# Inverse roots of the first four tiles by square root and reciprocal, one operand for the k and v weights, a last VectorE batch of four, and output stores on two queues

## The chip, the core and the metric

The kernel runs on one core of a Trainium2 chip. The metric is the time of one execution on the device, in microseconds (us); lower is better. The time of the kernel before is the median of three runs. Profiles show one further execution each, with their own time.

## What is computed

`x` has 2048 rows (tokens) of 512 numbers, in bf16. Two branches work on its layer-normalised form:

```python
xn = layernorm(x)                       # (x - mean) / sqrt(var + 1e-5)
q = (xn @ wq) as 32 heads of 16         # one k and one v for all heads
k, v = xn @ wk, xn @ wv                 # wk, wv: 512 x 16
p = softmax(q @ k.T * 16**-0.5)         # 32 heads x 2048 x 2048
s = (p @ v as 2048 x 512) @ wo
g = silu(silu(xn @ w1) @ w2)            # 512 -> 1792 -> 512
out = x + s * g
```

The exponentials of the softmax are by far the most elements: 32 x 2048 x 2048.

## The kernel before, in words

The five engines run programs that a planner inside the kernel file writes out. `Planner` (L108) keeps a clock for each engine; the code adds `Task`s with an engine, an expected duration, what they read and write and a priority, and the loop at L1856 always lets the engine with the lowest clock take its next task. The result is a fixed order for each engine, with semaphore waits where one engine needs another's result (`finalize`, L272; `run_engine`, L333). The expected durations only decide the order; on the chip each engine goes through its list as fast as its waits allow. The planner's thresholds are varied at random in each 6 us of planned time (`Mix.draw`, L349), from a list of seeds (`SEEDS`, L23; a seed of 0 leaves the base values). Another list of seeds, or another task, gives another order everywhere behind it.

**Exponentials.** The work is cut into 32 groups (16 blocks of queries and heads, twice) of 64 slots, so 2048 slots. One slot is a 128x512 block of scores that TensorE writes to one PSUM bank by four 64x32 matmuls (`score`, L1020). Each slot's exponential is made in one of two ways:

- On ScalarE (ACT): one `Exp` at L1804 over one bank, or over two banks at once, into `pa_sb`. TensorE then multiplies it with v, two matmuls a slot (L1382).
- On VectorE (DVE): one `tensor_scalar` at L1113 (L1833 for two banks) into `db_sb` makes bf16 bits of an approximate power. Three shifted copies of it, each over a whole batch, are added as integers on GpSimd (POOL, L1300) or, late in the run, on DVE (L1296), into `ds_sb`. All four are multiplied with differently weighted v and summed by TensorE, so a slot costs eight matmuls at L1382. Slots go to DVE in batches of `BS` = 8 (`pick_d`, L1080). A batch is begun only in a group with `MARGIN` (24, varied by the seeds) or more slots left, in the last group `MARGIN_END` (24). What is not taken by DVE goes to ACT.

**Start.** Four x tiles of 128 tokens are loaded first. DVE makes their mean and variance (L578, L582; tile 1 on ACT, L566 to L571), then the inverse root of variance + eps by a bit trick and two Newton steps: eight dependent DVE instructions a chain (L595 to L604), one chain for tiles 0 and 1, one for 2 and 3 (`FIRST`, L44), later ones for eight and four tiles. Then `xn` (L607), transposes on TensorE (L646), their evacuation (L656 on ACT, L657 on DVE), k by L681 and q by L793, then the first scores (L1035) and the first `Exp`. TensorE runs matmuls on zeros (L1757) until the first transposes. ACT's table load and a first `Exp` of one column stand at L557.

The k product takes 32 columns of weights for each quarter of the array from `wke_sb`, which ACT fills with eight copies of `wk` (L559). The evacuation of k multiplies with `part_sb`, a mask that keeps the first 16 rows of every other 32 and makes the others zero. The v product reads `wv_sb` (L719).

**End.** After the last `Exp` come the last products with v, the normalisation by DVE (L1403 to L1424), the last block of `wo` (L630), and for four output tiles r = 0 to 3 the gate and the residual: r = 0 and 1 by sums on TensorE (L1654) and a copy on ACT (L1657), r = 2 and 3 by an addition on DVE (L1668). Each then goes out by one 128 KB DMA from SyncE (SP) through `store` (L860, L861).

```python
tail["sums"] = [(r, part) for part in (1, 0) for r in PES]   # PES = (1, 0)
```

Of the kernel before, what the change touches and what calls it, by code (L numbers as in the profile page):

```python
# [15 lines left out]
P = 128  # L16
# [6 lines left out]
SEEDS, STRETCH = [0, 0, 107193, 696001, 868130, 0, 0, 145354, 0, 0, 0, 0, 659755, 570515, 0, 401028, 149754, 476048, 392543, 420941, 806026, 839768, 568520, 820467, 562019, 44193, 553940, 622483, 698310, 0, 0, 544188, 92220, 709879, 0, 0, 0, 801168, 299022, 0, 917407, 348101, 0, 418696, 641980, 788014, 105079, 62529, 143744, 620893, 549519, 710614, 527239, 0, 717222, 643687, 714474, 0, 598637, 596527, 685847, 646319, 190982, 346243, 377627, 0, 742035, 0, 484115, 974384, 0, 500386, 117077, 477174, 734943, 6340, 727301, 977691, 161521, 875247, 810658, 479061, 572316, 817044, 687626, 0, 340370, 623436, 215637, 14408, 0, 304983, 649749, 270166, 85731, 904261, 0, 0, 0, 0, 0, 9294, 415416, 179748, 0, 0, 265034, 0, 0], 6000.0  # L23
# [22 lines left out]
T_SP = 600.0  # L46
# [17 lines left out]
MARGIN, MARGIN_END = 24, 24  # L64
# [309 lines left out]
def bass_recurrent_scan__grouped_kv_mqa__dense_activation_silu__prompt_kernel(  # L374
# [29 lines left out]
    with ExitStack() as es:  # L404
# [6 lines left out]
        wk_sb = sb("wk_sb", [P, NDC, DH], BF16)  # L411
        wke_sb = sb("wke_sb", [P, NDC, P], BF16)
        wv_sb = sb("wv_sb", [P, NDC, DH], BF16)
# [72 lines left out]
        dma(SP, "wk", wk_sb[:], A_wk.rearrange("(dc p) e -> p dc e", p=P), 16, ["wk"], prio=0)  # L486
        dma(SP, "wv", wv_sb[:], A_wv.rearrange("(dc p) e -> p dc e", p=P), 16, ["wv"], prio=0)
# [19 lines left out]
        pl.add(Task(DV, 60.0, lambda v: v.memset(scr_sb[:], 0.0), (), ["scr"], -1))  # L507
# [41 lines left out]
        for e in (1, 0):  # L549
# [7 lines left out]
        pl.add(Task(AC, 1500.0, lambda a: a.activation(scr_sb[:, 0:1], scr_sb[:, 1:2], ACT.Exp), ["scr"], ["scr2"], 0))  # L557
        wke4 = wke_sb[:].rearrange("p c (i e) -> p c i e", e=DH)
        pl.add(Task(AC, 500.0, lambda a: a.activation(  # L559
            wke4, wk_sb[:, :, :].unsqueeze(2).to_broadcast([P, NDC, 8, DH]), ACT.Copy),  # L560
            ["wk"], ["wke"], 1, gate=lambda: "scr2" in pl.lastw and ("mv", 1) in pl.lastw))

# [24 lines left out]
        for n in first:  # L587
# [5 lines left out]
            def dv(fn, reads, writes, pre, ports=1):  # L593
                return pl.add(Task(DV, 66.0, fn, reads, writes, g, [pre] if pre is not None else [], ports=ports))
            t = pl.add(Task(DV, 66.0, lambda v, a=a, b=b, w=w: v.tensor_scalar(  # L595
                w, mv_sb[:, a:b, 1], LN_EPS, None, op0=ALU.add), [("mv", i) for i in tiles], [("ve", a)], g,
                [aggr[i] for i in tiles], ports=2))
            t = dv(lambda v, y=y, w=w: v.tensor_scalar(
                y.bitcast(I32), w.bitcast(I32), -0.5, RSQRT_M, op0=ALU.mult, op1=ALU.add), [("ve", a)], [("rs", a)], t, 2)
            for it, (c0, c1) in enumerate(RSQRT_C):  # L600
                t = dv(lambda v, y=y, h=h, c0=c0: v.scalar_tensor_tensor(
                    out=h, in0=y, scalar=c0, in1=y, op0=ALU.mult, op1=ALU.mult), [("rs", a)], [("vh", a)], t)
                t = dv(lambda v, w=w, h=h: v.tensor_tensor(h, h, w, ALU.mult), [("ve", a), ("vh", a)], [("vh", a)], t)
                t = dv(lambda v, y=y, h=h, c1=c1: v.scalar_tensor_tensor(  # L604
                    out=y, in0=h, scalar=c1, in1=y, op0=ALU.add, op1=ALU.mult), [("rs", a), ("vh", a)], [("rs", a)], t)
# [68 lines left out]
        def mk_K(c, ka, kb, bk=None):  # L674
            n = (kb - ka) * P

            def rnd(dc):
                def mk(b):
                    def emit(pe):
                        for j in range(4):  # L680
                            h = pe.matmul(bank(b)[32 * j:32 * (j + 1), 0:n], lhsT=wke_sb[:, dc, 32 * j:32 * (j + 1)],  # L681
                                          rhs=xnT_sb[:, dc, ka * P:kb * P], start=dc == 0, stop=dc == NDC - 1,
                                          tile_position=(0, 32 * j), skip_group_check=True)
                        return h
                    return emit
                return mk
# [20 lines left out]
            jb = job("K", c, 0.0, [(rnd(dc), ["wke"] + keys, max(64.0, n / 2.4 + 3.0)) for dc in range(NDC)], consume,  # L707
                     bk=bk, gate=lambda: all(k in pl.lastw for k in keys))
            if KU and n == NQ:
                product(jb, lambda k, rows, a, n: wke_sb[rows, k, a:a + n], lambda k, rows: xnT_sb[rows, k, ka * P:kb * P],  # L710
                        lambda k: ["wke"] + keys)

        def mk_V(c):
            def rnd(k):
                def mk(b):
                    def emit(pe):
                        for t in range(2 * k, 2 * k + 2):
                            for dc in range(NDC):
                                h = pe.matmul(bank(b)[:, t * DH:(t + 1) * DH], lhsT=xnT_sb[:, dc, (4 * c + t) * P:(4 * c + t + 1) * P],  # L719
                                              rhs=wv_sb[:, dc, :], start=dc == 0, stop=dc == NDC - 1, skip_group_check=True)  # L720
# [139 lines left out]
        def store(tt, t2):  # L860
            return pl.add(Task(SP, T_SP, lambda e: e.dma_start(of.rearrange("(t p) d -> p t d", p=P)[:, tt, :], ob_sb[:, tt % 4, :]),  # L861
# [188 lines left out]
        def pool_backlog():  # L1050
            return sum(t.dur for t in pl.tasks[PO] if t.dur == T_P64) + pl.clk[PO] - pl.clk[PE]
# [27 lines left out]

        def pick_d(t):  # L1080
            if st["assigned"] < 8 or any(k not in evac_kt or evac_kt[k].op is None for k in range(DK)):
                return None
            for bt in batches:
                for k in sorted(range(BS), key=lambda k: not mated(bt.g, k % 2)):
                    if k not in bt.slots and slot_time(bt.g, k % 2) <= t + 20:
                        return bt, k
            if any(len(bt.slots) < BS for bt in batches) or pool_backlog() > mix.P_HIGH:
# [848 lines left out]
```

## Time and profile before

| What | us |
|---|---|
| Median of three runs | 656.87 |
| Lowest and highest | 656.49, 657.04 |
| The profiled execution's own time | 657.56 |
| Its span, first to last instruction | 655.7 |
| Busy in it: TensorE (PE), ScalarE (ACT), VectorE (DVE), GpSimd (POOL) | 647.9, 641.0, 631.0, 576.5 |
| First `Exp` of scores starts | 12.00 |
| Last output store issued by | 653.78 |

A line of the profile's timeline has the start, the length of the piece, the engine, the line in the kernel, the operation, what it writes and reads, and how many instructions are merged in it; in brackets stands the idle time of the engine before it and what ended that. PEld is TensorE's loading of weights, SPq the queue on which SyncE issues DMAs. The granted TensorE clock is 1.0 in the whole span.

### The profile page before, as it was taken

The page shows a single profiled execution, that of the slowest core. Times are in us where ns is not written, and L with a number is a line of the kernel's source. Part 1 is how long each engine was busy: PE and PEld are TensorE (multiplying, and loading weights), DVE is VectorE, ACT ScalarE, POOL GpSimd, SP SyncE. Part 2 cuts the span into 40 slices and gives each one's busy share as a digit, 9 for nine tenths or more (in the row PEclk, how much of TensorE's full clock was granted, in tenths as well). Part 3 has the DMA queues.
Part 4 walks back from the last instruction along what each step waited for, and adds up shares of the span by engine and source line. Part 5 has one row for each costly group of instructions (what it writes and reads, how often), then busy time and mean ns, then how long its engine had stood idle before and what let it go on. Part 6 is the DMA issues. An engine that isn't in the chain of part 4 may idle for free.

```text
span 655.7 us, 44308 instructions
## 1 busy us (share of the span) xinstructions
PE 647.9 (99%) x21992; PEld 351.0 (54%) x19464; DVE 631.0 (96%) x1147; ACT 641.0 (98%) x1124; POOL 576.5 (88%) x330
## 2 busy tenths in 40 slices
PE   8999999999999999999999999999999999999997
PEld 4444456556544555554455556454665555665552
DVE  8999999999999999999999999999999999999992
ACT  6999999999999999999999999999999999999996
POOL 3069889999999999999999999999989999998950
PEclk9999999999999999999999999999999999999999
DMA  6521110000011210000000001000000001200001
GB/s 176 159 59 34 51 36 21 10 5 10 4 43 36 36 28 19 10 4 4 12 4 10 12 12 27 4 4 10 5 10 4 10 12 22 44 10 4 5 4 34
DMA packets 12937, 16.58 MB, mean 25 GB/s; under 512 B 2448, under 2 KB 11920, under 8 KB 12560
## 3 DMA queue, kind: packets, MB, share of 16 engines
q1 hardware_dynamic: 10544, 11.44, 5.9%
q0 software_dynamic: 1920, 2.03, 2.4%
q8 instruction: 162, 2.65, 1.7%
q10 hardware_dynamic: 288, 0.26, 0.1%
q14 instruction: 23, 0.19, 0.1%
HBM read 8.95 MB, written 3.67 MB: 19 GB/s over the span
## 4 chain that ended last, share of the span: by engine, by line
PE 86%; ACT 12%; DVE 2%; issue 0%
PE ps L1382 29%; PE ps L1035 25%; PE ps L757 18%; ACT pa_sb L1804 11%; PE ps L1029 11%; PE ps L1757 1%; DVE stats_sb L578 1%; PE ps L1614 1%; PE ps L646 0%; PE ps L681 0%; ACT t_sb L813 0%; PE ps L719 0%; DVE w_sb L852 0%; DVE xnT_sb L657 0%; DVE xn_sb L607 0%
## 5 line engine op out<-in xcount | busy, mean ns | idle before, releaser
L1804 ACT ACTIVATE pa_sb<-ps 128x512 bf16<-128x512 f32 (+1 forms) x1034 | 610.7, 765 | 3.3 <-PE ps L1035 2.8
L1300 POOL INT64_ADD ds_sb<-db_sb x298 | 562.2, 1961 | 29.6 <-DVE db_sb L1113 9.7
L1113 DVE TENSOR_SCALAR db_sb<-ps 128x512 uint16<-128x512 f32 x798 | 495.6, 680 | 3.8 <-PE ps L1035 1.0
L1035 PE MATMUL ps<-qt_sb,kt_sb 64*32 64x512 bf16 x5664 | 478.8, 378 | 0.7 <-DVE kt_sb L699 0.3
L1382 PE MATMUL ps<-ds_sb,v_sb 64*32 64x512 bf16 x4848 | 358.7, 376 | 0.0
L1382 PE MATMUL ps<-pa_sb,v_sb 64*32 64x512 bf16 x2480 | 264.4, 377 | 0.1
L1029 PE MATMUL ps<-qt_sb,kt_sb 64*32 64x512 bf16 x2528 | 243.7, 375 | 0.6 <-ACT pa_sb L1804 0.3
L1035 PEld LDWEIGHTS ps<-qt_sb,kt_sb 64*32 64x32 bf16 x5664 | 136.8, 89 | 141.0 <-ACT pa_sb L1804 55.9
L1382 PE MATMUL ps<-db_sb,v_sb 64*32 64x512 bf16 x1616 | 192.9, 376 | 0.0
L1382 PEld LDWEIGHTS ps<-ds_sb,v_sb 64*32 64x32 bf16 x4848 | 142.8, 91 | 44.4 <-issue 10.4
L757 PE MATMUL ps<-w_sb,u_sb 64*32 64x512 bf16 x1792 | 135.7, 377 | 0.0
L757 PE MATMUL ps<-xnT_sb,w_sb 64*32 64x512 bf16 x1792 | 135.2, 377 | 0.0
L1382 PEld LDWEIGHTS ps<-pa_sb,v_sb 64*32 64x32 bf16 x2480 | 91.1, 91 | 31.7 <-issue 10.8
L1382 PEld LDWEIGHTS ps<-db_sb,v_sb 64*32 64x32 bf16 x1616 | 64.5, 91 | 14.0 <-issue 2.4
L757 PEld LDWEIGHTS ps<-xnT_sb,w_sb 64*32 64x32 bf16 x1792 | 43.3, 91 | 24.2 <-issue 5.6
L757 PEld LDWEIGHTS ps<-w_sb,u_sb 64*32 64x32 bf16 x1792 | 46.2, 92 | 17.6 <-issue 4.8
L813 ACT ACTIVATE t_sb<-ps 128x512 bf16<-128x512 f32 x72 | 48.6, 674 | 0.0
L814 DVE SCALAR_TENSOR_TENSOR u_sb<-t_sb,ps 128x512 bf16<-128x512 bf16 x56 | 37.8, 675 | 1.1 <-ACT t_sb L813 0.9
L757 PE MATMUL ps<-xnT_sb,wq_sb 64*32 64x512 bf16 x480 | 37.7, 377 | 0.0
L1403 DVE STREAM_TRANSPOSE ps<-ps 128x512 f32<-128x512 f32 (+1 forms) x33 | 23.2, 707 | 12.1 <-PE ps L1382 12.1
L757 PE MATMUL ps<-wo_sb,on_sb 64*32 64x512 bf16 x384 | 29.6, 377 | 0.0
L1439 POOL DMA_DIRECT2D kt_sb<-kt_sb x4 | 2.3, 582 | 21.2 <-DVE kt_sb L699 15.8
(75 smaller groups left out, 195.0 us busy)
## 6 DMA issues: line engine op xcount, KB each, us to landing
w_sb<-in_B_w_dram SPq DMA_DIRECT2D x1, 1792.0 KB, 7.6
w_sb<-in_B_w_dram SPq DMA_DIRECT2D x14, 128.0 KB, 2.8
ds_sb<-in_A_x_dram SPq DMA_DIRECT2D x3, 512.0 KB, 6.6
qt_sb<-qt_sb SPq DMA_DIRECT2D x16, 96.0 KB, 2.2
out_dram<-in_A_x_dram SPq DMA_DIRECT2D x12, 128.0 KB, 2.4
out_dram<-ob_sb POOLq DMA_DIRECT2D x12, 128.0 KB, 3.2
v_sb<-v_sb SPq DMA_DIRECT2D x8, 80.0 KB, 2.2
wq_sb<-in_A_wq_dram SPq DMA_DIRECT2D x1, 512.0 KB, 4.9
```

The lines of the kernel that those rows point to most:

```text
L578: ts_ = pl.add(Task(DV, 593.0, lambda v, t=t: v.bn_stats(stats_sb[:, t, :], x_tile(t)), [xkey(t)], [("st", t)], 1 + j, gate=(lambda j=j: x ...
L757: h = pe.matmul(bank(b)[32 * j:32 * (j + 1), :], lhsT=lhs(k, rows, 32 * j, 32), rhs=rhs(k, rows), start=first, stop=last, tile_position=(r ...
L813: t1 = Task(AC, T_AF + 0.8333 * NQ, lambda a: a.activation(t_sb[:, k, :], bank(b), ACT.Tanh, scale=scale), [("ps", b)], [("t", k)], 0)
L814: t2 = Task(DV, T_P, lambda v: v.scalar_tensor_tensor(out=dst, in0=t_sb[:, k, :], scalar=1.0, in1=bank(b), op0=ALU.add, op1=ALU.mult), [(" ...
L1029: h = pe.add_instruction(mybir.InstMatmult(name=pe.bass.get_next_instruction_name(), engine=mybir.EngineType.PE, ins=[pe.lower_ap(q), pe.l ...
L1035: h = pe.matmul(to, lhsT=keys, rhs=q, start=True, stop=True, tile_position=(r0, 32 * j), skip_group_check=True)
L1113: bt.P[k] = pl.add(Task(DV, T_P, lambda v: v.tensor_scalar(db_sb[:, bt.b, k * NQ:(k + 1) * NQ], bank(b), 128.0 * LOG2E, 128.0 * (SHIFT_BET ...
L1300: whole["po"].append(pl.add(Task(PO, T_P64, lambda g: g.int64_add(ds_sb[:, s, :].bitcast(U64), db_sb[:, bt.b, :].bitcast(U64), words), rea ...
L1382: h = pe.matmul(bank(OB)[q:q + 32, :], lhsT=lhs(rows), rhs=rhs[rows], start=s0, stop=s1, tile_position=(64 * l, q), skip_group_check=True)
L1403: t1 = pl.add(Task(DV, (T_TR - 60.0) / parts + 60.0, lambda v, cols=cols: v.transpose(bank(OB)[:, cols], bank(OB)[:, cols]), [("ps", OB)], ...
L1614: h = pe.matmul(bank(tb[r])[32 * j:32 * (j + 1), :], lhsT=on_cols(oi % NON, slice(r0, r0 + 64), r * P + 32 * j, 32), rhs=wo_sb[r0:r0 + 64, ...
L1804: op = pl.place(AC, 0.8333 * NQ * n + T_AF, lambda a: a.activation(pa3[:, k0:k1 + 1:max(1, k1 - k0), :], ps3[:, b0:b1 + 1:step, :], ACT.Ex ...
```

## The change

Five edits, and a new list of seeds.

1. For tiles 0 to 3 the eight DVE instructions of a chain become two: ACT writes `sqrt(var + eps)` and DVE takes the reciprocal. The first table that ACT loads is the one for `Sqrt`; behind the second square root stands a one-column `Exp`, and with it the load of the table for `Exp`. Later tiles keep the old chain. A DVE memset writes eps to a column.
2. `wk` and `wv` are loaded side by side into one tile, `wkv_sb`. The k product reads its 32 columns (16 of k, 16 of v) directly, so ACT's eightfold copy is gone; the rows that now hold v are those that the mask makes zero. The k product waits for both loads.
3. A batch has its own size `bt.n`. In the last group a batch of four may be begun when no batch of eight fits any more and at least 14 slots are left (`MARGIN_4`); one of two would need 99, so it never is. Shifts of such a batch are half as wide.
4. The last four stores: r = 0 is issued by ACT, r = 1 and 2 go out as one DMA of 256 KB from SP, r = 3 alone from SP. The planner's duration of a store goes from 600 to 480 ns.
5. `pool_backlog`, a threshold of the planner, counts POOL tasks in another way.

```diff
-SEEDS, STRETCH = [0, 0, 107193, 696001, ...], 6000.0
+SEEDS, STRETCH = [0, 621430, 964855, 634377, ...], 6000.0
...
-T_SP = 600.0
+T_SP, T_ST = 600.0, 480.0
+FS, T_SQ, T_LD, PR_LD = 4, 210.0, 1500.0, 1
...
-MARGIN, MARGIN_END = 24, 24
+MARGIN, MARGIN_END, MARGIN_4, MARGIN_2 = 24, 24, 14, 99
...
+        eps = pl.add(Task(DV, 60.0, lambda v: v.memset(scr_sb[:, 3:4], LN_EPS), ["scr"], ["scr", "eps"], -1, [sc]))
...
-        pl.add(Task(AC, 1500.0, lambda a: a.activation(scr_sb[:, 0:1], scr_sb[:, 1:2], ACT.Exp), ["scr"], ["scr2"], 0))
-        wke4 = wke_sb[:].rearrange("p c (i e) -> p c i e", e=DH)
-        pl.add(Task(AC, 500.0, lambda a: a.activation(
-            wke4, wk_sb[:, :, :].unsqueeze(2).to_broadcast([P, NDC, 8, DH]), ACT.Copy),
-            ["wk"], ["wke"], 1, gate=lambda: "scr2" in pl.lastw and ("mv", 1) in pl.lastw))
+        pl.add(Task(AC, 1500.0, lambda a: a.activation(scr_sb[:, 0:1], scr_sb[:, 1:2], ACT.Sqrt if FS else ACT.Exp), ["scr"], ["scr2"], 0))
+        def wk2(k, rows):
+            return wkv_sb[rows, k, 0:2 * DH]
...
+            if a < FS:
+                t = pl.add(Task(AC, T_SQ, lambda q, w=w, a=a, b=b: q.activation(w, mv_sb[:, a:b, 1], ACT.Sqrt, bias=scr_sb[:, 3:4]),
+                                [("mv", i) for i in tiles] + ["eps"], [("ve", a)], -1, [aggr[i] for i in tiles] + [eps]))
+                if b >= FS:
+                    pl.add(Task(AC, T_LD, lambda q: q.activation(scr_sb[:, 0:1], scr_sb[:, 1:2], ACT.Exp), ["scr"], ["scr2"], PR_LD, [t]))
+                t = dv(lambda v, y=y, w=w: v.reciprocal(y, w), [("ve", a)], [("rs", a)], t)
...
-                            h = pe.matmul(bank(b)[32 * j:32 * (j + 1), 0:n], lhsT=wke_sb[:, dc, 32 * j:32 * (j + 1)],
+                            h = pe.matmul(bank(b)[32 * j:32 * (j + 1), 0:n], lhsT=wk2(dc, slice(0, P)),
...
-            return sum(t.dur for t in pl.tasks[PO] if t.dur == T_P64) + pl.clk[PO] - pl.clk[PE]
+            return sum(t.dur for t in pl.tasks[PO] if t.ports == 2) + pl.clk[PO] - pl.clk[PE]
...
+        def batch_size(g):
+            for n, least in ((BS, mix.MARGIN),) if g < NG - 1 else ((BS, MARGIN_END), (4, MARGIN_4), (2, MARGIN_2)):
+                if nleft[g] >= least and min(len(left[g, i]) for i in range(2)) >= n // 2:
+                    return n
+            return 0
...
+        def last_store(r, task):
+            tt = NT - 4 + r
+            if r == 0:
+                store(tt, task, AC)
+            elif r == 3:
+                store(tt, task)
+            else:
+                two[r] = task
+                if len(two) == 2:
+                    pl.add(Task(SP, T_ST, lambda e: e.dma_start(of.rearrange("(t p) d -> p t d", p=P)[:, NT - 3:NT - 1, :], ob_sb[:, 1:3, :]),
+                                [("ob", 1), ("ob", 2)], [("out", NT - 3), ("out", NT - 2)], 0, list(two.values()), dma=256 * 1024, on_place=outs.append))
```

81 lines of the change are left out of this document (41 added, 40 removed).

## The prediction

> **What bounds the kernel now.** First the page's busy rows, then the chain of waits near the end in order of time, then the table of busy time by stretch.
>
> ```profile
> span 655.7 us, 44308 instructions
> PE 647.9 (99%) x21992; PEld 351.0 (54%) x19464; DVE 631.0 (96%) x1147; ACT 641.0 (98%) x1124; POOL 576.5 (88%) x330
> ```
> ```profile
> 570.29 17.37 ACT pa_sb L1804 x30
> ...
> 633.43 11.07 ACT pa_sb L1804 x13
> 644.54 0.38 PE ps L1382
> ...
> 647.69 1.29 PE ps L1614 x24
> ...
> 652.31 0.42 DVE ob_sb L1668
> ```
> ```profile
> 30.00:570.00 540.00, 539.84 (x18879) 292.97 (x16691) 534.03 (x919) 538.14 (x960) 511.49 (x281) 1.00 0.08 19
> 570.00:633.00 63.00, 63.00 (x2232) 37.75 (x1951) 59.85 (x99) 62.86 (x107) 55.74 (x30) 1.00 0.05 11
> 633.00:647.30 14.30, 14.22 (x406) 6.70 (x351) 5.46 (x7) 14.24 (x17) 1.90 (x1) 1.00 0.01 3
> ```
>
> The columns after the stretch are PE, PEld, DVE, ACT, POOL, the granted clock (1.00), DMA share and GB/s. Up to 570 us every engine is nearly full: ACT 538.14 of 540, DVE 534.03. From 570.29 to 644.54 the chain is ACT's exponentials. In the last stretch DVE works 5.46 of 14.30 us and POOL 1.90, while ACT has no gap. So a microsecond comes off the time in three places: before the first exponential, in ACT's last stretch, and behind it.
>
> **Start: inverse roots.** The timeline of the start:
>
> ```profile
> 1.67 1.28 ACT L557 ACT_TABLE_LOAD   x1 [1.67 <-PEq L1921]
> 2.13 0.51 SPq L475 DMA_DIRECT2D wv_sb<-in_A_wv_dram  x1
> 2.96 0.20 ACT L557 ACTIVATE scr_sb<-scr_sb 128x1 f32<-128x1 f32 x1
> ...
> 5.25 0.19 ACT L571 ACTIVATION_READ_ACCUMULATOR pa_sb<-ds_sb,scr_sb 128x1 f32 x1
> 5.34 0.61 ACT L559 ACTIVATE wke_sb<-wk_sb 128x512 bf16<-128x512 bf16 x1
> 5.61 0.15 DVE L595 TENSOR_SCALAR var_sb<-mv_sb 128x2 f32<-128x2 f32 x1
> 5.67 0.24 DVE L582 BATCH_NORM_AGGREGATE mv_sb<-stats_sb 128x2 f32<-128x6 f32 x2
> ...
> 7.21 0.41 DVE L607 TENSOR_SCALAR xn_sb<-ds_sb,mv_sb,rstd_sb 128x512 bf16<-128x512 bf16 x1
> 7.61 1.05 DVE L607 TENSOR_SCALAR xn_sb<-ds_sb,mv_sb,rstd_sb 128x512 bf16<-128x512 bf16 x3
> 8.24 1.10 PEld L646 LDWEIGHTS ps<-ident,xn_sb 128*128 128x128 bf16 x16
> 8.88 1.08 ACT L656 ACTIVATE xnT_sb<-ps 128x512 bf16<-128x512 bf16 x2 [2.93 <-PE ps L646]
> 9.53 0.23 PEld L681 LDWEIGHTS ps<-xnT_sb,wke_sb 128*32 128x32 bf16 x16 [0.19 <-ACT xnT_sb L656]
> 10.00 1.28 DVE L578 BATCH_NORM_STATS2 stats_sb<-ds_sb 128x6 f32<-128x512 bf16 x2
> 12.00 2.98 ACT L1804 ACTIVATE pa_sb<-ps 128x512 bf16<-128x512 f32 x5 [0.50 <-PE ps L1035]
> ```
>
> The first chain starts at 5.61, a hop of 0.17 behind ACT's last sum for tile 1 (5.25 + 0.19 = 5.44), and its `xn` at 7.21: eight instructions, 1.60 us, interleaved with the second chain. By the new way a square root of two columns is bounded below by nothing and above by the 0.20 of an ACT instruction of one column; I take 0.20. The reciprocal: between 0.15 (L595, as small) and 0.20, L595 to `xn` being eight steps of 0.20; I take 0.20. So the square root runs 5.46 to 5.66, the reciprocal starts at 5.83, the first `xn` at about 6.05: 1.1 us earlier. The second pair's variances are there at 5.67 + 0.24 = 5.91; a hop, 0.20, a hop and a reciprocal make 6.65, while DVE is still busy with the first two `xn` (the last three are 0.35 apart), so the four end near 7.7 instead of 8.66. I take **1.0** for the transposes.
>
> The added waits: ACT's second square root waits for DVE; behind it in ACT's order stand the `Exp` load and then the evacuation at L656. A load and its one-column instruction took 1.28 + 0.20. From 6.25 that ends at 7.75, and the evacuation will be wanted at 8.88 - 1.0 = 7.88. ACT's idle time of 2.93 us hides the load, with about 0.1 us left; without that cover it costs up to 1.5. DVE's two reciprocals wait for ACT with the `xn` behind them, which is in the sum. The eps memset lies in DVE's work ahead of the statistics and could cost only a fraction of the table's smallest instruction; nothing taken.
>
> What is late next? The transposes themselves start at 8.24, though the first `xn` was ready at 7.62: TensorE still worked off its zero matmuls. The new order should hold fewer of them, since they stop at the planned time of `xn`; I carry the same lateness. Tiles 4 to 7 are wanted by L578, before at 10.00:
>
> ```profile
> L475 SPq DMA_DIRECT2D ds_sb<-in_A_x_dram x1: 632/632/632, 3.2 to 3.2; - x1
> ...
> DMA to landing us min/median/max: 5.8/5.8/5.8
> ```
>
> 3.2 + 5.8 is 9.0, exactly 1.0 earlier than their use: no more than 1.0 can be had. First exponential near 11.0. ACT has no work to wait for once it starts, so this 1.0 goes through to the end. Bounds 0 to 1.1.
>
> **k and v as one operand.** The K product still loads 16 times 128x32 weights. It now needs both loads:
>
> ```profile
> wv_sb<-in_A_wv_dram SPq DMA_DIRECT2D x1, 16.0 KB, 3.6
> ```
>
> 2.13 + 3.6 = 5.7 against 8.5 (9.53 - 1.0). The removed copy (0.61) lay in ACT's idle time, but it stood just where the square roots now run; alone it is worth nothing. 0.
>
> **Batch of four.** Rows of the exponentials, whole run (together, then by form), then ACT from 633.2 to 647.3, then DVE:
>
> ```profile
> L1804 ACT ACTIVATE pa_sb<-ps 128x512 bf16<-128x512 f32 (+1 forms) x1034 | 610.7, 765 | 3.3 <-PE ps L1035 2.8
> ```
> ```profile
> L1804 ACT ACTIVATE pa_sb<-ps 128x512 bf16<-128x512 f32 x828 | 440.0, 684 | 2.5 <-PE ps L1035 2.4
> L1804 ACT ACTIVATE pa_sb<-ps 128x1024 bf16<-128x1024 f32 x206 | 215.5, 1088 | 0.8 <-PE ps L1035 0.3
> ```
> ```profile
> L1804 ACT ACTIVATE pa_sb<-ps 128x1024 bf16<-128x1024 f32 x14 | 13.5, 1147 | 0.0
> L1804 ACT ACTIVATE pa_sb<-ps 128x512 bf16<-128x512 f32 x2 | 1.5, 748 | 0.0
> ```
> ```profile
> L1113 DVE TENSOR_SCALAR db_sb<-ps 128x512 uint16<-128x512 f32 x798 | 495.6, 680 | 3.8 <-PE ps L1035 1.0 <-POOL ds_sb L1300 0.7 <-PE ps L1029 0.2
> ...
> L1833 DVE TENSOR_SCALAR db_sb<-ps 128x1024 uint16<-128x1024 f32 x5 | 6.1, 1222 | 0.2 <-PE ps L1035 0.2
> ```
> ```profile
> 636.09 2.48 DVE L1296 TENSOR_SCALAR ds_sb<-db_sb 128x4096 uint16<-128x4096 uint16 x2
> 647.74 0.80 DVE L1403 STREAM_TRANSPOSE ps<-ps 128x256 f32<-128x256 f32 x2 [9.18 <-PE ps L1382]
> ```
>
> ACT has 828 + 2 x 206 = 1240 slots, DVE 798 + 2 x 5 = 808, 101 batches; together 2048. A slot costs ACT 610.7/1240 = 0.49 us. In the last stretch 14 x 2 + 2 = 30 slots fill its 14.24 us, so 0.47 each at most. Four slots fewer: 4 x 0.47 = 1.9. The batch costs DVE 4 passes of 501.7/808 = 0.62, 2.5 us, and three shifts of half of 1.24, 1.9 us: 4.4 us in a hole of 9.18; POOL could take shifts too. TensorE gets six more matmuls a slot, 24. At the middle's rate (18879 in 540 us, 0.029 us each) that is 0.7 us; the last stretch holds 406, 11.6 us at that rate of 14.3. So it fits, but the filler (L1614, ending 1.3 us after 647.69) must then find other holes. Between 1.9 (ACT alone decides) and 0 (all of it taken by TensorE and by waits for the last shift) I take **1.5**, nearer to the row of ACT, which sets the end.
>
> **Stores.** Timeline, landing, and the busiest half microsecond:
>
> ```profile
> 651.97 1.81 SPq L861 DMA_DIRECT2D out_dram<-ob_sb  x4
> ```
> ```profile
> DMA to landing us min/median/max: 1.7/1.8/1.8
> ```
> ```profile
> 653.50:654.00 0.50, 0.00 (x0) 0.00 (x0) 0.00 (x0) 0.00 (x0) 0.00 (x0) 1.00 0.80 268
> ```
>
> SP issues four in a row, the last from about 653.33 (1.81/4 = 0.45 each), though its data was there at 652.31 + 0.42 = 652.73. With two ahead of it gone from SP, it can go at 652.8: 0.55 earlier. But the DMA engines moved 268 GB/s, and 512 KB at that rate are 1.96 us; from the first issue at 651.97 they then end about as before. Bounds 0 and 0.55; I take **0.3**. The merged store waits for both rows and holds r = 3 behind it; r = 0 waits on ACT, with nothing behind it. The Trainium skill ("DMA: Bandwidth & Descriptors", section "Issuing engines are not separate DMA queues") says that DMAs issued from several engines run on the same 16 DMA engines, so that a second queue saves issue time alone. By that rule the end gains 0.55 at the most and the sum is at best -3.05; by the row's share of 0.80 a second queue could also fill the other fifth, and 1.96 us of transfer would become 1.6.
>
> **The redrawn order** of the middle: 0, since the rules there are unchanged. Doubles hold 412/1240 = 0.33 of all slots at 0.4925 us each and 28/30 = 0.93 of the last at about 0.465; 0.0275 over a share of 0.60 is 0.046 a slot, 0.09 us for a double. Twenty doubles more or fewer, a tenth of 206, make 1.8 us either way. That is my bound for it.
>
> **Sum**: -1.0 - 1.5 - 0.3 = -2.8. The profiled execution took 657.56 (655.7 of span and 1.9 around it), so 654.8; the median of the runs is 0.7 below the profiled one: **654.1**. Own range 652.3 to 655.9. A measurement can tell about 0.2% (1.3 us): faster is below 655.6, slower above 658.2.
>
> **Rivals.**
>
> *Slower: the new order gives DVE fewer batches.* Each batch of eight that the redrawn thresholds miss in the middle puts 8 x 0.49 = 3.9 us on ACT. For it: DVE has 6 us free in 540 and a batch needs 5 with its passes alone, so one is easily missed. Against: ACT and DVE are filled alike by the same rules. Saved elsewhere are 2.8, so it decides from the first batch: 808 + 4 - 8 = 804 slots give 654.1 + 3.9 = 658.0 (chance 0.06, within 0.2%); two or more batches, 662 (0.11).
>
> *One batch more*: 820 slots on DVE, 654.1 - 3.9 = 650.2. For it: the idle 6 us and POOL's 28. Chance 0.08.
>
> *The second table load is not hidden.* If a load behind running work takes twice the row's 1.28, it ends at 9.0, after the 8.88 of before: the 1.0 of the start is lost and 0.15 more. Then 655.3. The row of the first load shows nothing of this (its `Exp` follows at 2.96), but that load had no work ahead of it. The Trainium skill ("ScalarE: Activation LUTs", section "What ACT_TABLE_LOAD costs") gives 1283 ns for the load and about 1380 ns of draining for every switch to another set, 2.66 us; by that the time is 655.4, an estimate from that page. The trace agrees with the first figure (1.28), and no row here has a switch. Chance 0.09, half of it within 0.2%.
>
> *The batch is hidden anyway*: TensorE, with 24 matmuls more and 2 us less, becomes the end of the last stretch, and 1.5 becomes 0.3: 655.3. Chance 0.09, a third within 0.2%.
>
> **Chances.** Forecast 0.57 (0.03 of it within 0.2%). Faster: 0.54 + 0.06 + 0.06 + 0.08 = 0.74. Same: 0.03 + 0.03 + 0.03 + 0.06 = 0.15. Slower: 0.11. The range leaves out the extra batch (0.08) and two missed ones (0.11): 651.6, the sum with the middle's 1.8 and the bounds of the batch and the stores in its favour, to 658.1.
>
> **What would show it.** Right: first `Exp` at L1804 near 11.0; the second table load between 6.2 and 7.6 with the evacuation right behind; 812 slots on DVE and DVE's last hole down from 9.18 to some 4 us; ACT's last `Exp` about 2.5 us earlier; the last store issued as soon as the last L1668 ends. Wrong: the evacuation later than 8.5, a slot count other than 812, PEld waiting for nothing but its own queue before the last products, or the DMA rate of the end unchanged with the end no earlier.

## The result and the profile after

The changed kernel takes **654.31 us**, the median of eight runs (653.58 to 655.48). The kernel before took 656.49 in eight runs beside it (655.39 to 657.04). The ratio is 0.9972, with a 95% interval of 0.9961 to 0.9983: faster by 0.28%, or 1.8 us at that ratio and 2.2 by the medians. The forecast was 654.1. The profiled execution took 655.33, against 657.56 before, so the two profiles differ by the same 2.2 us as the medians. Two profiles of one kernel can differ by nearly as much (the changed kernel's span was 653.5 here and 651.7 in a later run on another chip), so below, times are compared by their ratios to the kernel before on the same chip, and profiles by distances inside each. Two executions of the experiments, of 746.43 and 1746.32 us, were slow ones and stand in none of the medians.

The page's busy rows after the change:

```profile
span 653.5 us, 44343 instructions
PE 644.5 (99%) x22007; PEld 347.8 (53%) x19480; DVE 632.8 (97%) x1136; ACT 640.9 (98%) x1132; POOL 578.6 (89%) x331
```

The span is 2.2 us shorter, and ACT's busy time is the same 641, with a second table load in it. So the 2.2 us have to be found by position, not in the totals. The timeline of the start:

```profile
5.08 0.19 ACT L568 ACTIVATION_READ_ACCUMULATOR pa_sb<-ds_sb,scr_sb 128x1 f32 x1
5.29 0.30 ACT L593 ACTIVATE var_sb<-mv_sb,scr_sb 128x2 f32<-128x2 f32 x1
5.62 0.17 DVE L597 RECIPROCAL rstd_sb<-var_sb 128x2 f32<-128x2 f32 x1
...
5.85 0.71 DVE L611 TENSOR_SCALAR xn_sb<-ds_sb,mv_sb,rstd_sb 128x512 bf16<-128x512 bf16 x2
5.97 0.30 ACT L593 ACTIVATE var_sb<-mv_sb,scr_sb 128x2 f32<-128x2 f32 x1 [0.38 <-DVE mv_sb L579]
6.28 1.28 ACT L596 ACT_TABLE_LOAD   x1
6.29 0.55 PEld L650 LDWEIGHTS ps<-ident,xn_sb 128*128 128x128 bf16 x8 [0.95 <-DVE xn_sb L611]
...
7.58 0.20 ACT L596 ACTIVATE scr_sb<-scr_sb 128x1 f32<-128x1 f32 x1
7.68 1.07 ACT L660 ACTIVATE xnT_sb<-ps 128x512 bf16<-128x512 bf16 x2
...
8.79 1.29 DVE L575 BATCH_NORM_STATS2 stats_sb<-ds_sb 128x6 f32<-128x512 bf16 x2 [0.47 <-DMA ds_sb<-in_A_x_dram]
...
10.79 0.60 ACT L1829 ACTIVATE pa_sb<-ps 128x512 bf16<-128x512 f32 x1 [0.50 <-PE ps L1039]
```

From the end of ACT's sum for tile 1 (5.08 + 0.19 = 5.27) to the first `xn` pass 0.58 us; before it was 7.21 - 5.44 = 1.77. The transposes start at 6.29 instead of 8.24. Two things then stand late. The load for `Exp` runs from 6.28 to 7.56, and the first evacuation (L660) follows with no idle time in brackets, so ACT kept the transposes waiting, and with them the first exponential. And DVE's statistics of tiles 4 to 7 now wait for the DMA (0.47). The first exponential starts at 10.79 instead of 12.00: **1.21 earlier**.

The table of busy time by stretch, columns as before:

```profile
30.00:570.00 540.00, 539.34 (x18939) 292.32 (x16768) 535.31 (x913) 537.32 (x961) 514.03 (x282) 1.00 0.09 19
...
633.00:647.30 14.30, 14.30 (x432) 6.64 (x364) 10.45 (x22) 11.43 (x16) 5.22 (x3) 1.00 0.01 3
```

In the last stretch DVE now works 10.45 us against 5.46, POOL 5.22 against 1.90, and ACT 11.43 against 14.24. The middle is as full as it was. The exponentials of the whole run, ACT's and DVE's, in both forms:

```profile
L1124 DVE TENSOR_SCALAR db_sb<-ps 128x512 uint16<-128x512 f32 x794 | 494.8, 682 | 6.3 <-PE ps L1039 3.7 <-PE ps L1033 0.5
...
L1829 ACT ACTIVATE pa_sb<-ps 128x512 bf16<-128x512 f32 x842 | 447.8, 693 | 2.4 <-PE ps L1039 1.9 <-PE ps L1033 0.5
...
L1829 ACT ACTIVATE pa_sb<-ps 128x1024 bf16<-128x1024 f32 x197 | 207.2, 1104 | 0.3
```
```profile
L1858 DVE TENSOR_SCALAR db_sb<-ps 128x1024 uint16<-128x1024 f32 x9 | 11.0, 1220 | 0.1
```

DVE has 794 + 2 x 9 = 812 slots and ACT 842 + 2 x 197 = 1236: one batch of four more on DVE, none lost, with nine doubles fewer on ACT. The end of the timeline, with ACT's last evacuation of the gate branch (L817) ahead of it; behind L817 ACT has nothing but exponentials until they are done:

```profile
622.79 0.73 ACT L817 ACTIVATE t_sb<-ps 128x512 bf16<-128x512 f32 x1
...
643.78 0.66 ACT L1829 ACTIVATE pa_sb<-ps 128x512 bf16<-128x512 f32 x1
...
644.55 2.93 PE L1625 MATMUL ps<-wo_sb,on_sb 64*32 64x512 bf16 x52
644.94 0.80 DVE L1414 STREAM_TRANSPOSE ps<-ps 128x256 f32<-128x256 f32 x2 [1.59 <-PE ps L1625]
...
646.25 0.49 DVE L1435 STREAM_TRANSPOSE on_sb<-otr_sb 128x128 f32<-128x128 f32 x2
647.40 0.56 PEld L634 LDWEIGHTS ps<-wo_sb,on_sb 128*32 128x32 bf16 x16 [0.42 <-issue]
647.41 1.05 PE L634 MATMUL ps<-wo_sb,on_sb 128*32 128x512 bf16 x16
...
649.98 0.40 SPq L1669 DMA_DIRECT2D out_dram<-ob_sb  x1
650.27 0.42 DVE L1693 TENSOR_TENSOR ob_sb<-w_sb 128x512 bf16<-128x512 bf16 x1
...
650.72 0.34 SPq L865 DMA_DIRECT2D out_dram<-ob_sb  x1
```

The last `Exp` ends at 643.78 + 0.66 = 644.44; the transposes behind it (L1414) start at 644.94, against 647.74 before: **2.80 earlier**, with DVE's hole down from 9.18 to 1.59. But the last block of `wo` (L634) starts at 647.41, 2.47 behind the transposes. Before, that distance was 1.71, because TensorE was free when the normalised rows came:

```profile
647.52 1.47 PE L1614 MATMUL ps<-wo_sb,on_sb 64*32 64x512 bf16 x24
...
649.45 1.05 PE L630 MATMUL ps<-wo_sb,on_sb 128*32 128x512 bf16 x16
```

Now 52 filler matmuls in a row (L1625, the products of the other `wo` blocks for the last tiles) stand in front of L634. Its weight load names "issue" as what ended the wait, not DVE's `on_sb`, which had been ready at 646.25 + 0.49 = 646.74: the queue of TensorE, not the data, was late. Against the kernel before, that gives **0.76 back**. The last addition ends at 650.69 against 652.73 (2.04 earlier), and the span ends 2.81 behind it against 2.97, so the stores brought **0.16**. The sum over the profiles is 1.21 at the start, 1.59 more by the transposes, less 0.76, and 0.16: 2.2 us. The 1.59 is not the batch's own worth, since it also holds whatever differs in the middle of the run, and there two profiles of the changed kernel itself differ by 1.85 (from the first exponential to L817 612.00 here, 610.15 in the later run). What the batch brings is read from the run without it, below.

The DMA rate in the last microseconds:

```profile
651.00:651.50 0.50, 0.00 (x0) 0.00 (x0) 0.00 (x0) 0.00 (x0) 0.00 (x0) 1.00 1.01 344
651.50:652.00 0.50, 0.00 (x0) 0.00 (x0) 0.00 (x0) 0.00 (x0) 0.00 (x0) 1.00 0.98 348
```

The DMA engines are now full at 344 to 348 GB/s, where they stood at a share of 0.80 and 268 GB/s.

### The profile page after: what moved, and what is told of

The parts are those of the page before. It is cut to its first block, busy times and chain, and to the rows that moved or that the text cites. A ratio compares the mean times of both kernels' runs of the same rounds, so it can differ in the third digit from the quotient of the medians.

```text
span 653.5 us, 44343 instructions
## 1 busy us (share of the span) xinstructions
PE 644.5 (99%) x22007; PEld 347.8 (53%) x19480; DVE 632.8 (97%) x1136; ACT 640.9 (98%) x1132; POOL 578.6 (89%) x331
## 3 DMA queue, kind: packets, MB, share of 16 engines
q8 instruction: 162, 2.65, 1.7%
## 4 chain that ended last, share of the span: by engine, by line
PE 96%; DVE 2%; DMA 1%; SPq 0%; issue 0%
PE ps L1393 33%; PE ps L1039 29%; PE ps L761 20%; PE ps L1033 13%; DMA ds_sb<-in_A_x_dram 1%; DVE stats_sb L575 1%; PE ps L650 1%; PE ps L1625 0%; PE ps L685 0%; SPq L474 0%; PE ps L723 0%; DVE w_sb L856 0%; DVE xn_sb L611 0%; DVE mv_sb L579 0%; DVE w_sb L859 0%
## 5 line engine op out<-in xcount | busy, mean ns | idle before, releaser
L1393 PE MATMUL ps<-pa_sb,v_sb 64*32 64x512 bf16 x2472 | 258.0, 377 | 0.0
L1393 PE MATMUL ps<-db_sb,v_sb 64*32 64x512 bf16 x1624 | 189.5, 376 | 0.0
L1393 PEld LDWEIGHTS ps<-ds_sb,v_sb 64*32 64x32 bf16 x4872 | 140.6, 91 | 41.8 <-issue 12.1
L761 PE MATMUL ps<-w_sb,u_sb 64*32 64x512 bf16 x1792 | 132.7, 377 | 0.0
L1393 PEld LDWEIGHTS ps<-pa_sb,v_sb 64*32 64x32 bf16 x2472 | 87.9, 91 | 28.2 <-issue 10.2
L1393 PEld LDWEIGHTS ps<-db_sb,v_sb 64*32 64x32 bf16 x1624 | 62.1, 91 | 13.0 <-issue 3.4
L761 PEld LDWEIGHTS ps<-w_sb,u_sb 64*32 64x32 bf16 x1792 | 44.5, 91 | 17.3 <-issue 4.0
L817 ACT ACTIVATE t_sb<-ps 128x512 bf16<-128x512 f32 x72 | 48.8, 677 | 0.6 <-PE ps L761 0.5
L761 PE MATMUL ps<-xnT_sb,wq_sb 64*32 64x512 bf16 x480 | 36.1, 377 | 0.0
L1414 DVE STREAM_TRANSPOSE ps<-ps 128x512 f32<-128x512 f32 (+1 forms) x33 | 23.2, 707 | 4.3 <-PE ps L1393 2.7
```

The lines of the kernel that those rows point to most:

```text
L761: h = pe.matmul(bank(b)[32 * j:32 * (j + 1), :], lhsT=lhs(k, rows, 32 * j, 32), rhs=rhs(k, rows), start=first, stop=last, tile_position=(r ...
L817: t1 = Task(AC, T_AF + 0.8333 * NQ, lambda a: a.activation(t_sb[:, k, :], bank(b), ACT.Tanh, scale=scale), [("ps", b)], [("t", k)], 0)
L1393: h = pe.matmul(bank(OB)[q:q + 32, :], lhsT=lhs(rows), rhs=rhs[rows], start=s0, stop=s1, tile_position=(64 * l, q), skip_group_check=True)
L1414: t1 = pl.add(Task(DV, (T_TR - 60.0) / parts + 60.0, lambda v, cols=cols: v.transpose(bank(OB)[:, cols], bank(OB)[:, cols]), [("ps", OB)], ...
```

## The experiments

The theory: the time comes from the start (about 1 us) and from the last batch, less what the filler takes back; the stores bring little. The rivals: the redrawn order alone makes the difference; the second table load eats the start; the tail hides the batch. Of the twelve kernels the first four ran on one chip, the next four on a second and the last four on a third. The kernel before, run beside them, had medians of 655.56, 655.87 and 655.54.

**The batch of four taken out of the changed kernel.**

```diff
-MARGIN, MARGIN_END, MARGIN_4, MARGIN_2 = 24, 24, 14, 99
+MARGIN, MARGIN_END, MARGIN_4, MARGIN_2 = 24, 24, 99, 99
```

> The changed kernel with the batch of four switched off (808 slots on DVE instead of 812), everything else and the seeds as in the changed kernel. Theory (the batch takes 1.9 us of exponentials off ACT's last stretch and gives 0.7 back to the late filler of TensorE): 1.0 to 1.4 us slower than the changed kernel's 654.3, so 655.3 to 655.7, with the last Exp 2 us later and the filler gone from the path. Rival (the last stretch gained by the redrawn order, not by the batch): within 0.3 us of the changed kernel.

654.73 us, ratio 0.9994 [0.9985, 1.0003]. Against 0.9974 for the next kernel, which has the batch and ran on the same chip, that is 0.0020 or 1.3 us lost (0.9 by the medians), with about 0.9 us of uncertainty by the two intervals. The end of its timeline:

```profile
620.47 0.73 ACT L817 ACTIVATE t_sb<-ps 128x512 bf16<-128x512 f32 x1
...
644.43 0.80 DVE L1414 STREAM_TRANSPOSE ps<-ps 128x256 f32<-128x256 f32 x2 [7.19 <-PE ps L1393]
...
646.37 1.05 PE L634 MATMUL ps<-wo_sb,on_sb 128*32 128x512 bf16 x16
```

Up to L817 the engines have done the same work as in the changed kernel, so distances from there can be compared, and they repeat well: from L817 to the transposes 22.15, to L634 24.62, in the changed kernel's profile above, in its later one and in the next run. Without the batch they are 23.96 and 25.90. So the batch brings the transposes **1.81** forward, and **1.28** of it is left at L634: the distance between the two is 1.94 without the batch and 2.47 with it, so the filler takes 0.53 of the batch's gain. The other 0.23 of the 0.76 (1.94 against 1.71) stands without the batch too. DVE's hole is back to 7.19.

What the new seeds, the start and the stores leave without the batch is 0.0006, 0.4 us, with an interval that holds both nothing and 0.65, the lower of two values for the start's own worth (below). The batch is worth about 1.3 us in this order; that the redrawn order alone makes the difference falls.

**The old stores in the changed kernel.** The body of the function becomes one line; the planner's 480 ns stay.

```diff
-            tt = NT - 4 + r
...
+            store(NT - 4 + r, task)
```

> The changed kernel with the four last stores as before, one each, all from SP. Theory (the DMA engines set the end, so the queues save little): 0.2 us slower than the changed kernel, 654.5; the span behind the last addition 2.97 us as before instead of 2.81. Rival (the issue time counts in full): 0.55 us slower, 654.9.

653.79, ratio 0.9974 [0.9964, 0.9983]: the same as the changed kernel's 0.9972. SP's queue, on which the four stores are issued:

```profile
648.33 2.02 SPq L865 DMA_DIRECT2D out_dram<-ob_sb  x4
```

SP issues until 650.35, and the span (652.2) ends 3.1 behind the last addition (649.09) instead of 2.8. In the profile the edit is worth 0.2 to 0.3 us; in the time it can't be told from nothing.

**The batch of four alone in the kernel before** (edits 3 and 5, old seeds).

```diff
-MARGIN, MARGIN_END = 24, 24
+MARGIN, MARGIN_END, MARGIN_4, MARGIN_2 = 24, 24, 14, 99
```

> The kernel before with the batch of four alone, seeds as before. Theory: 0.9 to 1.3 us faster than before (1.9 off ACT, some given back by TensorE's filler), about 655.4. Rival (the order that the old seeds give in the last group leaves no good place for the batch; the gain needs new seeds): 0 to 0.3 us faster.

655.47, ratio 1.0000 [0.9991, 1.0009]: nothing, and my number was wrong. Its timeline says where it went:

```profile
631.27 0.63 ACT L813 ACTIVATE t_sb<-ps 128x512 bf16<-128x512 f32 x1
...
644.93 2.76 PE L1621 MATMUL ps<-wo_sb,on_sb 64*32 64x512 bf16 x48
645.15 0.80 DVE L1410 STREAM_TRANSPOSE ps<-ps 128x256 f32<-128x256 f32 x2 [4.84 <-PE ps L1389]
...
647.62 1.05 PE L630 MATMUL ps<-wo_sb,on_sb 128*32 128x512 bf16 x16
```

Against the next kernel, which has no batch and ran on the same chip (L813 at 631.49, transposes at 646.43, L630 at 648.14), counted from L813, the last `Exp` ended 1.77 earlier (at 643.94 and 645.93), the transposes came 1.06 earlier (13.88 against 14.94) and L630 only 0.30 (16.35 against 16.65): TensorE was late with its products, and 48 filler matmuls, which had lain in ACT's last stretch, now stand between the transposes and L630. In the old order the tail takes most of the batch's gain, as the rival said, and 0.30 is too little to see in the time.

**The stores alone in the kernel before** (edit 4, old seeds).

```diff
-                    out_task[tt] = store(tt, t2)
+                    last_store(r, t2)
```

> The kernel before with the new stores alone. Theory: 0.2 us faster than before, the span behind the last addition 2.8 us instead of 2.97. Rival (issue time in full): 0.55 us faster. Nothing else in the order moves.

655.64, ratio 0.9999 [0.9990, 1.0008]. In its profile the last addition ends at 651.42 and the span at 654.2, 2.8 behind it instead of 2.97: 0.2 in the profile, none that the time can show.

**The changed kernel again**, without an edit, on the second chip, to be set beside the next three.

> The changed kernel once more, unaltered, so that the next three can be read against it on one chip. All theories: 0.28% (1.8 us) faster than before, within 0.1%.

653.65, ratio 0.9967 [0.9955, 0.9979]. On this chip, too, the change is worth 0.3%.

**The old chain, with the changed kernel's order held.** The eight old instructions take the place of the first reciprocal, for all four tiles at once; square roots, second reciprocal and second load are gone, and eight zero matmuls are put back. The rest of each engine's list stays as the changed kernel has it.

```diff
+    gone = sq + [TAGS["ld"].op, rc[1]]
...
+        pl.order[op.eng].remove(op)
...
+        then(v.tensor_scalar(w, mv, LN_EPS, None, op0=ALU.add))
+        then(v.tensor_scalar(y.bitcast(I32), w.bitcast(I32), -0.5, RSQRT_M, op0=ALU.mult, op1=ALU.add))
...
+    rc[0].emit = chain
```

> The changed kernel with every engine's order held, but the first four inverse roots by the old eight DVE instructions (one chain for all four tiles, behind the last variance), no square roots on ACT, no second table load, and eight more zero matmuls on TensorE. Theory (what the start gains goes through to the end): first xn near 7.5 and first Exp near 12.1 instead of 10.8, and the whole 1.2 to 1.4 us slower than the changed kernel. Rival (the engines catch up in the crowded stretch behind the start, or wait for x tiles anyway): at most 0.4 us slower.

654.82, ratio 0.9986 [0.9977, 0.9995], so 0.0019 or 1.25 us slower than the changed kernel beside it (1.2 by the medians), with about 1 us of uncertainty. ACT's timeline:

```profile
11.67 2.98 ACT L1834 ACTIVATE pa_sb<-ps 128x512 bf16<-128x512 f32 x5 [0.50 <-PE ps L1044]
```

The first `Exp` is 0.85 later than the 10.82 of the kernel beside it, not 1.3 as expected. The order is the same, so a later start by itself reaches the end; whether 0.85 or more of it does, the time can't tell.

**No table to switch.** `Identity` with a factor of 20 stands where the square root was, so that the table for `Exp` serves from the start; the inverse roots are then not roots.

```diff
-        pl.add(Task(AC, 1500.0, lambda a: a.activation(scr_sb[:, 0:1], scr_sb[:, 1:2], ACT.Sqrt if FS else ACT.Exp), ["scr"], ["scr2"], 0))
+        pl.add(Task(AC, 1500.0, lambda a: a.activation(scr_sb[:, 0:1], scr_sb[:, 1:2], ACT.Exp), ["scr"], ["scr2"], 0))
...
-                t = pl.add(Task(AC, T_SQ, lambda q, w=w, a=a, b=b: q.activation(w, mv_sb[:, a:b, 1], ACT.Sqrt, bias=scr_sb[:, 3:4]),
+                t = pl.add(Task(AC, T_SQ, lambda q, w=w, a=a, b=b: q.activation(w, mv_sb[:, a:b, 1], ACT.Identity, scale=20.0, bias=scr_sb[:, 3:4]),
```

> The changed kernel, order held, with a straight line (scale and bias) in place of the square root, so that there is one table for the whole run and no second load; it leaves out the root of the first four tiles. Theory (the second table load stands in front of the first evacuation, which its transposes would allow at about 6.9 instead of 7.68): first Exp 0.7 us earlier, near 10.1, and the time 0.5 to 0.7 us less. Rival (the load is hidden, as the prediction had it): first Exp within 0.1 us and no change.

653.60, ratio 0.9964 [0.9951, 0.9977], against 653.65 and 0.9967 for the changed kernel beside it: no gain that can be told. ACT's timeline, then DVE's:

```profile
6.05 0.29 ACT L593 ACTIVATE var_sb<-mv_sb,scr_sb 128x2 f32<-128x2 f32 x1 [0.38 <-DVE mv_sb L579]
6.25 0.18 ACT L596 ACTIVATE scr_sb<-scr_sb 128x1 f32<-128x1 f32 x1
6.81 1.08 ACT L660 ACTIVATE xnT_sb<-ps 128x512 bf16<-128x512 bf16 x2 [0.38 <-PE ps L650]
...
10.31 1.08 ACT L1829 ACTIVATE pa_sb<-ps 128x512 bf16<-128x512 f32 x2 [0.50 <-PE ps L1039]
12.49 2.49 ACT L1829 ACTIVATE pa_sb<-ps 128x512 bf16<-128x512 f32 x4 [1.09 <-PE ps L1039]
```
```profile
9.52 1.29 DVE L575 BATCH_NORM_STATS2 stats_sb<-ds_sb 128x6 f32<-128x512 bf16 x2 [1.11 <-DMA ds_sb<-in_A_x_dram]
...
11.38 0.60 DVE L703 TENSOR_SCALAR kt_sb<-ps,part_sb 128x384 bf16<-128x384 f32 x1
```

Without the load the evacuation starts 0.9 earlier (7.72 in the kernel beside it), so the load had stood in front of it by 0.9. The first `Exp` is 0.5 earlier, and then ACT idles 1.09: the next scores need L703, which stands on DVE behind the statistics of tiles 4 to 7, and these wait for the DMA until 9.52. In this profile the tiles landed late: in the kernel beside it the statistics start at 8.63, though there, too, DVE waited 0.27 for them. An estimate from these rows: with the tiles there at 8.63, the next `Exp` would start 12.49 - 9.52 = 2.97 later, at 11.60, where the kernel beside it ends its second `Exp` at about 11.90 (10.82 and the same 1.08). So the load was not hidden, but by this estimate taking it away brings only about 0.3, because the x tiles are late next; the time can't show so little.

**Filler moved behind the last blocks of the tail.** Three of the four blocks at L634 go ahead of the last of the twelve filler products.

```diff
+    late = fill[11:]
...
+    pe.extend(rest[:0] + last[:3] + late + last[3:] + rest[0:])
```

> The changed kernel with TensorE's last 16 block products in another order: the last blocks of output tiles 0 to 2 go ahead of the last filler product (that of tile 3) instead of behind all twelve. Same work. Theory (the filler holds TensorE until 647.4 while the last block is ready at 646.75): the last block starts 0.5 us earlier and the time falls by 0.2 to 0.5 us. Rival (behind it ACT's three evacuations and the chain of tile 3 set the end): less than 0.1 us.

653.68, ratio 0.9967 [0.9955, 0.9979]: the same as the changed kernel. Its timeline behind the last transposes:

```profile
643.15 0.80 DVE L1414 STREAM_TRANSPOSE ps<-ps 128x256 f32<-128x256 f32 x2 [1.59 <-PE ps L1625]
...
645.40 0.83 PE L634 MATMUL ps<-wo_sb,on_sb 128*32 128x512 bf16 x12
```

L634 starts 2.25 behind the transposes, against 2.47 in the changed kernel beside it (643.12 and 645.59). Eleven of the twelve products still stand ahead of the block, so 0.2 is all that the move gives it, too little to see in the time. It does not tell whether the filler is to blame.

**The start alone in the kernel before, with its order held.** Two square roots, the load and two reciprocals take the place of the chains; eight zero matmuls go; ACT's copy of `wk` stays, between the two square roots.

```diff
+    ac[k:k + 1] = [roots[0], copy, roots[1], load]
...
+    dv.insert(dv.index(xn[1]) + 1, recs[1])
```

> The kernel before with every engine's order held, and only the first four inverse roots by square root and reciprocal: two square roots on ACT (the copy of wk between them), the second table load behind, two reciprocals on DVE in place of 16 instructions, eight zero matmuls fewer. Theory (the start's gain goes through to the end): first Exp near 11.0 instead of 12.0 and the whole 0.8 to 1.2 us faster than before. Rival (it shows only in the order drawn for it): less than 0.4 us faster.

654.93, ratio 0.9990 [0.9981, 0.9999]: 0.65 us faster, with 0.6 of uncertainty, so between the theory and the rival. ACT's timeline:

```profile
5.54 0.61 ACT L562 ACTIVATE wke_sb<-wk_sb 128x512 bf16<-128x512 bf16 x1
6.06 0.28 ACT L1936 ACTIVATE var_sb<-mv_sb,scr_sb 128x2 f32<-128x2 f32 x1
...
10.86 3.90 ACT L1811 ACTIVATE pa_sb<-ps 128x512 bf16<-128x512 f32 x6 [0.50 <-PE ps L1042]
```

The first `Exp` is where the changed kernel has it (10.79 and 10.82), with the copy still there: it lies between the square roots while the second waits for its variances anyway (6.06 here, 5.97 and 6.00 without the copy). So one operand for k and v is worth 0.1 at most.

**No filler on one half of the tail.** The twelve products of the late filler are left out.

```diff
+    gone = [op for op in pl.order[PE] if "tail_half.<locals>.emit" in op.emit.__qualname__ and op.lane == 0]
...
+        pl.order[PE].remove(op)
```

> The changed kernel, order held, without TensorE's twelve late filler products of one row half (L1625, lane 0); it leaves out half of three of the four blocks of wo for the last four output tiles. Theory (the filler takes back part of what the batch of four gains): the last block starts 0.45 us earlier, right behind the last transpose of DVE, and the time falls by 0.3 to 0.5 us. Rival (as in the run with another order of the tail, the end behind it absorbs it): less than 0.15 us.

652.77, ratio 0.9954 [0.9942, 0.9967]: 0.0013 to 0.0018 below the changed kernel on two other chips (0.9967, 0.9972), 0.8 to 1.2 us, with about 1 us of uncertainty. That is more than the 0.3 to 0.5 expected. The end of its timeline:

```profile
642.78 0.80 DVE L1414 STREAM_TRANSPOSE ps<-ps 128x256 f32<-128x256 f32 x2 [1.60 <-PE ps L1393]
...
644.45 1.05 PE L634 MATMUL ps<-wo_sb,on_sb 128*32 128x512 bf16 x16 [1.69 <-DVE on_sb L1435]
```

The last block now waits for `on_sb` itself, 1.67 behind the transposes, as in the kernel before (1.71) and not 2.47. So the filler is what stood in front of it, and 0.8 is what it takes back. The run leaves that work out, so 0.8 is what could be had at most if it found an earlier place.

**The seeds exchanged**, two kernels: the changed kernel with the old list, and the kernel before with the new list.

```diff
-SEEDS, STRETCH = [0, 621430, 964855, 634377, ...], 6000.0
+SEEDS, STRETCH = [0, 0, 107193, 696001, ...], 6000.0
```

> The changed kernel with the seeds of before, all five edits kept. Theory (the edits pay only with an order drawn for them, since a list of seeds fits one sequence of decisions): 3 us or more slower than the changed kernel, so slower than before. Rival (the edits pay whatever the order): still faster than before.

> The kernel before with the seeds of the changed kernel, no edit. Theory (as above): 3 us or more slower than before. Rival (the new seeds are simply better): faster than before by 1 us or more.

659.89, ratio 1.0062 [1.0048, 1.0076], and 660.69, ratio 1.0078 [1.0065, 1.0092]: the first 0.9% slower than the changed kernel with its own list (1.0062/0.9972), the second 0.8% slower than the kernel before: 6 and 5 us, as the theory had it. Groups of the first of them by form, then its end:

```profile
L1829 ACT ACTIVATE pa_sb<-ps 128x512 bf16<-128x512 f32 x932 | 489.6, 710 | 3.0 <-PE ps L1039 2.2 <-PE ps L1033 0.3
...
L1829 ACT ACTIVATE pa_sb<-ps 128x1024 bf16<-128x1024 f32 x150 | 160.3, 1106 | 0.1
```
```profile
641.98 2.96 ACT L1829 ACTIVATE pa_sb<-ps 128x1024 bf16<-128x1024 f32 x4
...
649.60 0.80 DVE L1414 STREAM_TRANSPOSE ps<-ps 128x256 f32<-128x256 f32 x2 [5.17 <-PE ps L1393]
```

All five edits are in its code, and its first `Exp` starts at 10.70. But in this order the batch of four is never begun: ACT has 932 + 2 x 150 = 1232 slots, so DVE has 816, which are 102 batches of eight, one more than in the kernel before. ACT has 150 doubles instead of 197, with the singles longer (710 ns against 693), and its last `Exp` ends at 641.98 + 2.96 = 644.94 while the transposes start at 649.60: TensorE works off products for 4.7 us behind ACT, where the changed kernel has 0.5. So one batch more on DVE did not make this kernel faster; its order costs more than the batch can bring.

The second kernel has 808 slots on DVE, as the kernel before has with its own list, and 178 doubles instead of 206. TensorE is hardly late there (1.05 from the end of the last `Exp` to the transposes, against 0.50 in the kernel before with its own list). So a list costs time on the other's tasks in more than one way, and what in the lists does it was not taken apart.

## Why the prediction was right

Direction and size were right: 654.1 was forecast and 654.31 measured, and of the -2.8 that the sum gave, -2.2 came. That the two times agree within 0.2 is partly luck, since the kernel before took 656.49 beside it and not the 656.87 that the forecast started from. Step by step:

- **Start, predicted -1.0.** The profile shows -1.21; in the time it is -0.65 (put into the kernel before) to -1.25 (taken out of the changed one), with 0.6 and about 1 us of uncertainty by their intervals. The chain was sized well: 0.61 foreseen from ACT's sum to the first `xn`, 0.58 measured. Two errors cancel in it: the square root takes 0.30, above the bound of 0.20 that I took from a one-column instruction, and the hop from it to the reciprocal is 0.03 (5.59 to 5.62) and not 0.17. "I carry the same lateness" of the transposes failed: they start at 6.29 and not at 7.24, right behind the first `xn`, with 12 zero matmuls instead of 20. For the same reason "with about 0.1 us left" failed: the evacuation was wanted near 6.8, and the load stood 0.9 in front of it. The evacuation still started at 7.68, near the 7.88 of the forecast: the transposes came about as much too early as the load held them up, which is luck. It is the load, then, that sets the first exponential. The x tiles, which I took as the limit, are the next thing late, about 0.3 behind it by the estimate above. My bound of 1.0 from their landing was a little too tight: they were there at 8.79 and not at 9.0.
- **The rival of the second load** was right that the load is not hidden (0.9, above), but its cause falls, and the start is not lost. Behind running work, too, the load takes 1.28, as the first one does, and it starts 0.01 behind the square root. Square root to one-column `Exp` is 1.61 from start to start with it and 0.20 without: 1.4 for the whole switch. The Trainium skill ("ScalarE: Activation LUTs", section "What ACT_TABLE_LOAD costs") gives 1283 ns and about 1380 ns of draining; the first figure agrees (1.28), and no second 1.38 stands in these rows.
- **One operand for k and v, predicted 0.** Right: with the copy kept between the square roots, the first `Exp` starts at 10.86, against 10.79 and 10.82 without it.
- **Batch of four, predicted -1.5, with 0 to -1.9 as bounds.** It is -1.28 in the profiles, counted from L817, and -0.9 to -1.3 in the time, with 0.9 of uncertainty; 812 slots came as foreseen. The 1.9 of ACT was sized well (1.81 at the transposes). The brake, "the filler must then find other holes", was named, but in the sum it had only 0.4 (1.9 less 1.5), and 0.53 was measured; with the 0.23 that is there without the batch it makes the 0.76. One of the prediction's own signs of being wrong came true with it: the weight load of the last block waits for nothing but its own queue. DVE's hole shrank to 1.59 and not to some 4, since DVE works 5.0 us more in the last stretch and the hole ends 2.8 earlier. In the old order the brake took nearly all (0.30 left, ratio 1.0000): what the batch pays depends on where the order puts TensorE's late work.
- **Stores, predicted -0.3.** 0.16 in the profile, 0.2 to 0.3 in the kernels that have or lack only them, not measurable in the time. That the end could use the idle fifth of the DMA engines was right (268 to 348 GB/s). But each store then takes longer to land, 2.1 to 2.2 us, against 1.7 to 1.8 before and 1.8 to 2.0 in the changed kernel with the old stores, and this eats most of it. The rule of the Trainium skill that I weighed ("DMA: Bandwidth & Descriptors", section "Issuing engines are not separate DMA queues"), by which only issue time is saved, is not refuted by this: the four stores before were issued over 1.81 us, which is about 290 GB/s for 512 KB, so issue alone may have held them at 268, and the gain is below the 0.55 of issue time. No run tells the second queue from the merged store.
- **The redrawn order, predicted 0 within 1.8.** Start, batch and stores make -2.65 in the profiles (1.21, 1.28 and 0.16), and -2.2 came, so 0.45 was lost elsewhere; in the middle two profiles of one kernel differ by more than that, so whether the order cost it is open. The reason given, "the rules there are unchanged", was not the right one: the same rules with the other list of seeds cost 0.8 to 0.9%, 5 to 6 us, so each list fits its own tasks and not the other's. The bound of 1.8, from twenty doubles, was too narrow for an order that is not drawn for its edits: 47 doubles fewer went with TensorE 4.7 us late at the end. What a newly drawn list would bring to the kernel before, without the edits, no run shows.
- **Fewer batches, one more batch**: neither came; 812 slots in 102 batches.

No kernel here that does all the work is measurably faster than the changed one. The 0.8 us of the filler is the only gain that the runs point to, and where that work could stand earlier was not found.

## What to carry to other kernels

Before an engine is relieved near the end of a kernel, look at what fills the others while it works: work that was free as filler comes onto the path as soon as the engine that covered it is done earlier, and that is taken off the gain. When a chain at the start is shortened, ask at every step which input comes next from memory; here the table load was not hidden, but the x tiles came late right behind it, so hiding it would have brought about 0.3 us by estimate. An order that was drawn for one set of tasks is worth more than small edits to these tasks (5 to 6 us against 2.2 here), so an edit is judged with an order drawn for it, and its own worth by holding the order. Where two profiles vary in the middle by as much as an edit is worth, count from the last point up to which both have done the same work.

## What the hardware showed beside that

- A switch of ACT's table from `Sqrt` to `Exp` takes 1.28 us for the load behind running work, and about 1.4 in all (1.61 from square root to `Exp` with it, 0.20 without).
- A square root of two columns with a column as its bias takes 0.28 to 0.30 us; an `Exp` of one column takes 0.18 to 0.20.
- Four stores of 128 KB issued one after the other from one queue kept the DMA engines at a share of 0.80 and 268 GB/s at most; one of 256 KB and two of 128 KB on two queues reached 1.0 and 348 GB/s, with 2.1 to 2.2 us from issue to landing instead of 1.7 to 2.0.
